# A forgetting-attention plus SwiGLU kernel: list-scheduled order, attention output with queries on partitions, q and k turned by DMA

## The chip, the cores and the metric

The kernel runs on one core of one Trainium2 chip. The metric is the device time of one execution in microseconds (us). The profile is one execution recorded by the hardware profiler; its span, from the first to the last instruction, is 1.5 to 2.5 us shorter than the timed figure of the same execution. The granted clock is the share of the full TensorE clock that the profile records (0.5 is half clock). The engines are PE (matmul; PEld is its weight load, which overlaps PE), DVE (VectorE), ACT (ScalarE), POOL (GpSimd) and SP (SyncE, which here only issues DMAs). A run over 1.5% above the fastest run of its own kernel is called slow and left out of ratios.

## The reference, cut to what matters

```python
B, H, S, D = 8, 8, 576, 64                       # q, k, v: float32, (B, H, S, D)
scores = q @ k^T / sqrt(D)
cum    = cumsum(log(clip(f, 1e-4, 1)))           # f: (B, H, S), 0.8 to 1.0
scores = where(causal, scores + cum[i] - cum[j], -1e9)
attn   = softmax(scores)
x      = (attn @ v) as (B*S = 4608 tokens, H*D = 512)
out    = (silu(x @ w_gate) * (x @ w_val)) @ w_out   # 512 -> 1536 -> 512, float32 weights
```

q and k are drawn with a scale of 0.1, so q.k/8 has a standard deviation of about 0.1 x 0.1 x 8 / 8 = 0.01, while one step of `cum` averages about 0.1. The scores are therefore almost all decay.

## The kernel before

Each head is scored in four slots; keys lie on partitions in the scores, so `pt = exp(scores)` is already the right operand for attention times V. V is stationary and `pt` moves. The output has the 64 features of a head on partitions plus a 65th row, the row sum (V carries columns of ones). Since the sum of a query then lies in a row, dividing by it needs it on 64 partitions: for most heads it travels by DMA, is inverted, goes out to DRAM and comes back broadcast. For the first 256 queries of batch 0 PE turns it in f32.

```python
def transposes(p, nm):                  # q and k of every pair of heads: six PE transposes each
    for n in range(QT):
        nc.tensor.transpose(t[:, n * QP : n * QP + P], src[:, n], ident)

def straighten(p, nm, a, eng):          # then four copies per pair, on ACT or DVE
    ...

def pv(h, i):                           # V stationary (128x128), up to 320 columns of pt move
    for n, (kt, q0, w) in enumerate(BANKS[i]):
        nc.tensor.matmul(o[:, q0 - q_lo : q0 - q_lo + w], VB[b][:, kt, j, :], PT[h, half][:, c : c + w], ...)
    ...
    if on_act: nc.scalar.activation(dst, o[: D + 1, :q_n], AF.Copy)
    else:      nc.vector.tensor_copy(dst, o[: D + 1, :q_n])

def collect(x, g, lo, n):               # the row sums of four heads onto 128 partitions
    nc.scalar.dma_start(out=SC[x][:, :c], in_=E[g][D : D + 1, ...])
def recip(x, n):   nc.vector.reciprocal(...)
def back(x, n):    nc.scalar.dma_start(out=rc_dram[...], in_=RC...)
def spread(x, n):  nc.scalar.dma_start(out=RB[x]..., in_=rc_dram[...].to_broadcast([D, GH * n]))
def normalise(x, h, lo, n):
    nc.vector.tensor_mul(xT[...], E[g][:D, c : c + n], RB[x][...])
... (cut: loads, casts on POOL, decay rows, exp, mask)

for h in range(BH):                     # a fixed order by slots; FFN matmuls are dealt out between them
    for i in range(NSLOT):
        at(slot(h, i), qk, h, i)
        ...
```

The score matmul has 68 rows of contraction: 64 of q and k, and four rows that carry the decay (`cum` in pieces that bfloat16 can hold, and ones).

The softmax here doesn't subtract the row's maximum and nothing guards it: scores larger than these inputs give would overflow.

## Time and profile before

| | before |
|---|---|
| median of 4 runs | 451.49 us (451.31 to 451.66) |
| span of the profiled run | 449.0 us |
| PE / DVE / ACT / POOL busy | 93 / 64 / 59 / 39% |
| sum of all matmuls at full rate | 391.9 us |
| loss (span less that sum) | 57.1 us |

The first lines are from the page of the kernel before: busy time by engine, then two of the rows that cut the span into 40 slices of 11.2 us. A digit is a busy share in tenths; DMA is the busy share of the 16 DMA engines.

```profile
PE 418.1 (93%) x2818; PEld 248.2 (55%) x2818; DVE 289.1 (64%) x523; ACT 267.1 (59%) x551; POOL 174.6 (39%) x409
...
PE   8399587899899899999999999999999999999996
...
DMA  9899960762818644942594359425912222200201
```

PE stands at 8 or 9 tenths from the eighth slice to the last but one. The second fence is from the timeline of PE, at 253 us: start, length, line, shapes, number of matmuls.

```profile
253.42 0.50 PE L135 MATMUL tp<-ident,b_q 128*128 128x128 bf16 x6
253.76 0.59 PE L311 MATMUL fo<-wo,hh 128*128 128x512 bf16 x2
```

Six matmuls of 128 columns start at 253.42 and the next group starts 0.34 us later: 57 ns each (55.6 on average in full streaks; a 512-column matmul takes 215.7). The Trainium skill ("TensorE: Matmul & The Clock Gate", Back-to-back issue gap) gives N/2.4 + 2.5 ns for a warm, isolated gap; this trace agrees with that formula, with about 2.2 to 2.4 ns as the constant. So the cost of PE work at full clock can be written down from its columns alone. I call the sum of columns/2.4 + 2.2 ns over all matmuls, dummies left out and four times the columns for f32, the matmul sum. (The four is an assumption. The 16 f32 transposes of 128 columns ran at half clock, with 214 ns from the first to the second of each pair, which would be twice the columns. Counted so, the sum before is 1.7 us smaller and the loss before 1.7 us larger.) What the span has beyond the sum is the loss: waits, half clock, start and end. The cumulative loss at a time is that time less the matmul sum of what had started by then.

Next, the busy time of each engine by window (window, length, PE busy with its instruction count, then the other engines; at the end granted clock, DMA share, GB/s), and two steps of the chain of waits that ended last, cut to the first 60 us (start, length, what).

```profile
20.00:40.00 20.00, 18.53 (x111) 12.29 (x110) 11.30 (x31) 10.03 (x21) 10.49 (x23) 0.56 1.18 208
40.00:60.00 20.00, 14.14 (x123) 10.71 (x121) 9.24 (x21) 11.36 (x24) 12.38 (x28) 0.91 1.17 210
```

```profile
41.40 11.44 DMA nat_q<-in_q_dram
52.92 6.87 DMA sc<-ev
```

By 80 us the loss is already 41.8 us of 57.1. From 20 to 60 us the DMA share is above 1 (the profile adds up the times of packets, so it can pass 1), and the chain steps through loads and then the 6.87 us of the row sums' DMA.

Last, groups of instructions from the page: line, engine, operation, output<-inputs, shapes, count | busy us, mean ns | idle time before, and what ended it.

```profile
L166 PE MATMUL s<-QK 68*128 68x320 bf16 (+4 forms) x448 | 88.5, 268 | 8.8 <-DMA QK<-dec_d 5.8
...
L198 PE MATMUL o<-pt,VB 128*128 128x320 bf16 (+4 forms) x448 | 88.0, 267 | 5.6 <-DVE QK L144 2.6
...
L219 DVE COPY ev<-o 65x320 f32<-65x320 f32 (+1 forms) x68 | 32.5, 478 | 42.2 <-PE o L198 42.1
...
L142 ACT ACTIVATE QK<-tp 64x576 bf16<-64x576 bf16 x66 | 42.6, 645 | 13.5 <-DMA nat_q<-in_q_dram 4.0
```

L166 are the scores, L198 attention times V, L219 half of the evictions of its output (the copies of a matmul's output from its PSUM tile to SBUF), L142 half of the straightening copies after the PE transposes.

### The profile page before, as it was taken

Reading aid. Unit: us, or ns where it says so; the run is one execution under the profiler, and the core shown is the slowest. Engines: PE = TensorE matmul, PEld = TensorE weight load, DVE = VectorE, ACT = ScalarE, POOL = GpSimd, SP = SyncE. Lnnn points to the kernel's source line nnn. Section 1 sums busy time; section 2 is a strip of 40 time slices with the busy share of each in tenths; the row PEclk is TensorE's granted clock in tenths of the full one; section 3 lists DMA queues with packets and bytes.
Section 4 is the critical chain, followed back from the end, with each engine's and each line's share of the span. In section 5 each row is a group of like instructions: output and inputs, shape, how many; then the busy total and the mean of one; then the engine's idle time right before and its main releaser. Section 6 shows DMA issues by size and latency. Waiting matters only on the chain.

```text
span 449.0 us, 8044 instructions
## 1 busy us (share of the span) xinstructions
PE 418.1 (93%) x2818; PEld 248.2 (55%) x2818; DVE 289.1 (64%) x523; ACT 267.1 (59%) x551; POOL 174.6 (39%) x409
## 2 busy tenths in 40 slices
PE   8399587899899899999999999999999999999996
PEld 3256465676766565555555555555555554444562
DVE  6464466585866875797379737973796479386280
ACT  5446466666667778776677667766776643233231
POOL 7855654334245646444444444444444310000000
PEclk9758999999999999999999999999999999999999
DMA  9899960762818644942594359425912222200201
GB/s 210 175 231 202 223 142 12 196 142 49 193 55 197 149 110 131 213 95 70 154 208 99 69 155 205 102 70 153 207 29 64 88 54 54 85 10 1 93 2 70
DMA packets 70195, 53.52 MB, mean 119 GB/s; under 512 B 45834, under 2 KB 64266, under 8 KB 69322
## 3 DMA queue, kind: packets, MB, share of 16 engines
q1 hardware_dynamic: 57626, 38.94, 35.0%
q10 hardware_dynamic: 6704, 9.34, 8.9%
q0 software_dynamic: 5824, 4.72, 6.8%
q8 instruction: 22, 0.36, 0.4%
q14 instruction: 19, 0.16, 0.1%
HBM read 47.38 MB, written 10.17 MB: 128 GB/s over the span
## 4 chain that ended last, share of the span: by engine, by line
PE 75%; DMA 9%; DVE 7%; ACT 4%; issue 2%; SPq 1%; ACTq 1%; POOL 0%; DVEq 0%; POOLq 0%
PE fo L311 20%; PE gp L293 18%; PE vp L302 18%; PE o L198 8%; PE s L166 8%; PE tp L135 4%; DMA nat_q<-in_q_dram 3%; DMA nat_v<-in_v_dram 3%; DVE th L296 2%; DVE xT L274 2%; DMA sc<-ev 2%; DVE hh L304 1%; ACT th L295 1%; ACT QK L142 1%; ACT pt L172 1%
## 5 line engine op out<-in xcount | busy, mean ns | idle before, releaser
L172 ACT ACTIVATE pt<-s 128x384 bf16<-128x384 f32 (+2 forms) x256 | 127.6, 502 | 77.1 <-PE s L166 72.0
L181 POOL TENSOR_SCALAR_AFFINE_SELECT pt<-pt 128x128 bf16<-128x128 bf16 (+2 forms) x256 | 83.8, 328 | 180.3 <-ACT pt L172 177.1
L302 PE MATMUL vp<-xT,wv 128*128 128x512 bf16 (+2 forms) x528 | 125.4, 341 | 1.4 <-DVE hh L304 1.4
L293 PE MATMUL gp<-xT,wg 128*128 128x512 bf16 (+2 forms) x528 | 125.9, 342 | 0.8 <-DVE th L296 0.5
L296 DVE SCALAR_TENSOR_TENSOR th<-th,gp 128x512 f32<-128x512 f32 (+2 forms) x132 | 77.5, 587 | 66.6 <-ACT th L295 63.6
L311 PE MATMUL fo<-wo,hh 128*128 128x512 bf16 x432 | 107.2, 379 | 0.8 <-DVE th L296 0.8
L166 PE MATMUL s<-QK 68*128 68x320 bf16 (+4 forms) x448 | 88.5, 268 | 8.8 <-DMA QK<-dec_d 5.8
L295 ACT ACTIVATE th<-gp 128x512 f32<-128x512 f32 (+2 forms) x132 | 68.3, 517 | 47.1 <-PE gp L293 39.0
L198 PE MATMUL o<-pt,VB 128*128 128x320 bf16 (+4 forms) x448 | 88.0, 267 | 5.6 <-DVE QK L144 2.6
L304 DVE TENSOR_TENSOR hh<-th,vp 128x512 bf16<-128x512 f32 (+2 forms) x132 | 77.5, 587 | 9.3 <-PE vp L302 0.7
L166 PEld LDWEIGHTS <-QK 68*128 68x128 bf16 x448 | 44.4, 101 | 49.4 <-issue 8.1
L302 PEld LDWEIGHTS <-wv 128*128 128x128 bf16 x528 | 49.3, 98 | 33.5 <-issue 2.4
L293 PEld LDWEIGHTS <-wg 128*128 128x128 bf16 x528 | 49.4, 98 | 32.2 <-issue 1.2
L219 DVE COPY ev<-o 65x320 f32<-65x320 f32 (+1 forms) x68 | 32.5, 478 | 42.2 <-PE o L198 42.1
L311 PEld LDWEIGHTS <-hh 128*128 128x128 bf16 x432 | 39.3, 97 | 35.6 <-issue 1.2
L144 DVE COPY QK<-tp 64x576 bf16<-64x576 bf16 x62 | 46.6, 752 | 17.7 <-PE tp L135 16.9
L198 PEld LDWEIGHTS <-VB 128*128 128x128 bf16 x448 | 39.2, 98 | 23.2 <-issue 4.9
L142 ACT ACTIVATE QK<-tp 64x576 bf16<-64x576 bf16 x66 | 42.6, 645 | 13.5 <-DMA nat_q<-in_q_dram 4.0
L274 DVE TENSOR_TENSOR xT<-ev,rb 64x576 bf16<-64x576 f32 (+2 forms) x72 | 48.6, 675 | 2.9 <-DMA rb<-rc_d 1.9
L314 ACT ACTIVATE ot<-fo 128x512 f32<-128x512 f32 x36 | 21.5, 596 | 29.9 <-PE fo L311 28.3
L122 POOL CAST b_q<-nat_q 96x768 bf16<-96x768 f32 x32 | 27.1, 846 | 6.7 <-DMA nat_q<-in_q_dram 6.7
L122 POOL CAST b_k<-nat_k 96x768 bf16<-96x768 f32 x32 | 27.0, 843 | 0.9 <-DMA nat_k<-in_k_dram 0.9
(49 smaller groups left out, 176.2 us busy)
## 6 DMA issues: line engine op xcount, KB each, us to landing
nat_q<-in_q_dram SPq DMA_DIRECT2D x32, 288.0 KB, 3.8
nat_k<-in_k_dram SPq DMA_DIRECT2D x32, 288.0 KB, 4.2
out_dram<-ot SPq DMA_DIRECT2D x36, 256.0 KB, 2.1
nat_v<-in_v_dram SPq DMA_DIRECT2D x64, 128.0 KB, 5.7
rb<-rc_d ACTq DMA_DIRECT2D x12, 576.0 KB, 6.8
wg<-in_moe_w_gate_dram POOLq DMA_DIRECT2D x4, 384.0 KB, 13.2
wv<-in_moe_w_val_dram POOLq DMA_DIRECT2D x4, 384.0 KB, 15.2
wo<-in_moe_w_out_dram POOLq DMA_DIRECT2D x4, 384.0 KB, 9.6
```

The costliest lines, as they stand in the source:

```text
L122: nc.gpsimd.tensor_copy(BF[nm, p % 2][:QP].rearrange("p t h d -> p h t d"), nat.pop((nm, p)).rearrange("p h (t d) -> p h t d", d=D),)
L166: nc.tensor.matmul(s[:, c : c + w], QK[b][:, 2 * j + 1, kt * P : (kt + 1) * P], QK[b][:, 2 * j, q0 : q0 + w], start=True, stop=True,)
L172: nc.scalar.activation(pt[:, off : off + c], s[:, :c], AF.Exp, scale=0.125)
L181: nc.gpsimd.affine_select(out=diag, in_=diag, pattern=pat, compare_op=ALU.is_ge, fill=0.0, base=0, channel_multiplier=-1,)
L198: nc.tensor.matmul(o[:, q0 - q_lo : q0 - q_lo + w], VB[b][:, kt, j, :], PT[h, half][:, c : c + w], start=(i <= 1 and n == 0), stop=(last a ...
L274: nc.vector.tensor_mul(xT[a * D : (a + 1) * D, (h % H) // 2, b0 : b0 + n], E[g][:D, c : c + n], RB[x][:, j * n : (j + 1) * n])
L293: nc.tensor.matmul(g_[:, :n], wg[:, ko, fs], xT[:, ko, ts], start=(ko == 0), stop=(ko == KD - 1))
L295: nc.scalar.activation(th[:, :n], g_[:, :n], AF.Tanh, scale=0.5)
L296: nc.vector.scalar_tensor_tensor(out=th[:, :n], in0=th[:, :n], scalar=1.0, in1=g_[:, :n], op0=ALU.add, op1=ALU.mult)
L302: nc.tensor.matmul(v_[:, :n], wv[:, ko, fs], xT[:, ko, ts], start=(ko == 0), stop=(ko == KD - 1))
L304: nc.vector.tensor_mul(h_[:, :n], th[:, :n], v_[:, :n])
L311: nc.tensor.matmul(o[:m], hh[fc][:, m0 : m0 + m], wo[:, fc, :], start=(fc == 0), stop=(fc == KF - 1))
```

## The change

The intent is fewer columns through PE and less work around it. Attention times V gets its operands swapped: a 128x128 block of probabilities is stationary and 65 columns of V (64 and ones) move. As before, blocks above the diagonal are not computed. The output then has queries on partitions and the row sum as a column, so a reciprocal and a broadcast multiplication on DVE normalise it with no DMA. The price is five PE transposes per pair of heads to bring x back to features on partitions. q and k of batches 2 to 7 are cast to bfloat16 by a DRAM-to-DRAM DMA (issued by POOL, `narrow`) and turned by 96 DMA transposes (issued by SP, `turned`; called crossbar transposes here), in place of POOL casts and PE transposes. A list scheduler (`Plan`) simulates engines, buffers and DMA with modelled durations at build time, and fixes the order of each engine's instructions. The diff is cut to its core and condensed; the comments are added here.

```diff
-for h in range(BH):                       # slots
-    for i in range(NSLOT):
-        at(slot(h, i), qk, h, i)
+class Plan:                               # list scheduler: heap of events, one queue per engine
+    def op(self, eng, fn, after=(), take=(), use=(), key=0.0, ready=0.0, dma=None): ...
+    def run(self, idle=None):
+        ...
+        lanes = [0.0] * 8                 # DMAs of SP and ACT in flight
... (cut)
-def transposes(p, nm): ...                # for every pair of heads
+def narrow(e, b, x):                      # batches 2 to 7, f32 -> bf16, DRAM to DRAM
+    nc.gpsimd.dma_start(out=qk_dram[2 * b + x, :HSD]..., in_=(q, k)[x][b]...)
+def turned(e, p, j, x):                   # each row: 64 values of its token, 64 of what follows
+    src = bass.AP(qk_dram.tensor, qk_dram.offset + lo, [[D, S], [1, P]])
+    nc.sync.dma_start_transpose(out=QK[:, hqk[p].i, 2 * j + x, :S], in_=src)
+def rows(e, p):                           # decay rows then overwrite partitions 64 to 67
+    E[e].dma_start(out=QK[D:KR, hqk[p].i, :, :S], in_=dec_dram[:, 2 * p : 2 * p + 2]...)
... (cut)
-nc.tensor.matmul(o[:, q0 - q_lo : q0 - q_lo + w], VB[b][:, kt, j, :], PT[h, half][:, c : c + w], ...)
+for n, (kt, qb, c) in enumerate(cells):   # 15 cells per head
+    lo = base + qb * (D + 1)
+    nc.tensor.matmul(o[:, lo : lo + D + 1], pt[:, c : c + P], VB[hvb[b].i][:, kt, hb, : D + 1], ...)
-def collect / recip / back / spread / normalise   # row sums by DMA
-def turn / turn_back                              # row sums by f32 PE transposes
+def invert(e, bo, br, n):
+    nc.vector.reciprocal(RC[br.i][:, :n].unsqueeze(2), o[:, :, D:])
+def scale(e, bo, br, bx, j, qb, nq):
+    nc.vector.tensor_mul(XN[bx.i][...], o, r)          # r: the reciprocal, broadcast over 64 columns
+def flip(e, bx, bt, qb, nq):
+    for n in range(nq):
+        nc.tensor.transpose(t[:, n * P : (n + 1) * P], XN[bx.i][:, qb + n]..., ident)
... (cut: buffers now share xT and wo; decay rows of batches 0 and 1 by four DMAs, one per row)
+W_AT = [15.0, 19.0, 36.0, 42.0]           # planned times at which weights are fetched
```

## The prediction

> **What bounds the kernel now.** TensorE. The page gives PE 93% busy against DVE 64%, ACT 59%, POOL 39%, and the chain that ended last is 75% PE. From 200 to 430 us PE is never idle (busy time by windows) and the matmuls stand back to back: starts in the timeline are 215.7 ns apart at 512 columns, 138 at 320, 55.6 at 128, 28 at 64. That is N/2.4 GHz plus about 2.3 ns[...]; weight loads are hidden, also behind 64 columns. That spacing summed over all matmuls but the 18 dummies gives 392 us of the 449 us span. The other 57 us are lost to waits and half clock: 42 us in the first 80 us (DMA-bound: about 205 GB/s at share 0.9 to 1.2; clock 0.5 to 0.6 from 20 to 40 us), 10 us from 80 to 200 us, about 5 us at the end.
>
> **What the change does to PE.**
> - Attention times V: the probabilities become stationary, V with its ones column moves. Per head 15 matmuls of 65 columns replace 7 of 1600 columns in all: at 29 to 31 ns each 0.45 us against 0.69 us. 64 heads: 44 to 29 us, -15 us.
> - q and k transposes: 384 to 96 of 128 columns, 55.6 ns each: -16 us.
> - New output transposes, 160: +9 us. The f32 turns for row sums vanish: -7 us.
> - 37 output tiles instead of 36: +2.6 us. Scores and gates unchanged (45 and 187 us).
> Sum: 392 to about 368 us, all critical while PE is dense.
>
> **Off PE.** ACT loses the evictions of o (21 us) and most straightening copies; DVE loses 31 us of evictions and most of 47 us of copies, gains reciprocals, scales and xT copies (my estimate 65 us). Both stay under 70%. POOL loses 48 of 64 q/k casts. DMA gains 12 DRAM-to-DRAM casts (1.2 MB read each) and 96 crossbar transposes of 147 KB (14 MB). The skill ("Advanced Engine Details and Errata", X-Bar Transpose) calls those as fast as ordinary DMAs; no run here shows it. The DMA share after 90 us is 0.1 to 0.9, so there is room, and attention leads the FFN, so a late transpose has slack.
>
> **Ramp.** The bytes needed first (q, k, v of two batches, weights) are the same, so it stays DMA-bound. The row-sum chain goes (a 6.9 us wait in the chain at 53 us), and a list order fills gaps. I expect 48 us of loss instead of 57. The static order rests on modelled durations, slightly short for ACT (0.55 us modelled, 0.595 measured at 512 columns); small PE waits are in that.
>
> **Prediction.** Span 368 plus 48 to 51, plus 2.4 us by which the timed run exceeds the profile: 420 us; 8 in 10 between 409 and 437. Faster by over 2%: 0.91, within 2%: 0.06, slower: 0.03.
>
> **Right or wrong in the profile.** The 65-column matmuls' starts 28 to 32 ns apart; PE full from about 100 us to the end; about 24 us less warm matmul work; loss before 80 us of 35 to 42 us; the last pairs' transposes landing before PE wants them.
>
> **What would make it wrong.** Runs of up to nine 65-column matmuls, each with its own weight load, going at 55 ns (+23 us: then within 2%); crossbar transposes taking several us of queue or DMA each, so scores wait for QK after 100 us; a static order that blocks PE behind exp, mask or the single o and t banks.

## The result, and the profile after

The kernel after takes 425.21 us (median of 4 runs, 423.55 to 428.66) against 451.49 us. The ratio is 0.9424, with a 95% interval of 0.9381 to 0.9466. Here and below a ratio is the mean time of one kernel's fast runs over that of the other's in the same rounds, so not quite the ratio of the medians. The result is correct. The change is faster by about 5.8%.

The same page lines of the kernel after (slices of 10.6 us):

```profile
PE 388.1 (91%) x3071; PEld 227.5 (54%) x3114; DVE 230.3 (54%) x438; ACT 215.1 (51%) x442; POOL 126.9 (30%) x351
...
PE   3626999989999869999999999999999999999996
...
DMA  9994799966693798569959959975401002001002
```

| | before | after |
|---|---|---|
| span of the profiled run, us | 449.0 | 424.4 |
| matmul sum, us | 391.9 | 368.1 |
| loss, us | 57.1 | 56.3 |
| first score matmul at, us | 13.2 | 35.9 |
| cumulative loss at 40 / 80 / 140 / 160 us | 27.7 / 41.8 / 47.8 / 50.5 | 35.2 / 41.0 / 42.6 / 50.1 |

(The trace of the kernel after lacks 43 of the FFN's matmul records. The sum takes them from the program, so it is not affected; PE's busy figure is.)

So of the 24.6 us that the span lost, 23.8 are matmul columns that are no longer there, and only 0.8 are saved waiting (22.1 and 2.5 with f32 at twice the columns). That the loss hardly changed is partly luck, for gains and losses of several us cancel in it. Within the loss there is movement: the new kernel loses 7.5 us more in the first 40 us, 12.7 us less from 40 to 140 us, and 4.8 us more from 140 to 160 us. Two new problems can be seen in the PE row: the digits 3, 6, 2, 6 at the start, and the single 6 in the fifteenth slice, at about 150 us; the kernel before has no digit under 8 between its seventh slice and its last.

The windows of the kernel after:

```profile
20.00:40.00 20.00, 7.50 (x70) 5.80 (x68) 6.24 (x11) 5.84 (x14) 3.23 (x7) 0.61 0.67 119
40.00:60.00 20.00, 18.91 (x246) 15.20 (x245) 14.04 (x34) 18.01 (x45) 12.96 (x39) 0.88 0.94 171
...
120.00:160.00 40.00, 34.97 (x320) 20.82 (x323) 16.82 (x36) 22.64 (x48) 14.93 (x44) 0.97 0.81 132
```

From 20 to 40 us PE did 7.50 us of work, against 18.53 before (part of which was at half clock and on row sums), while the DMA share fell to 0.67 from 1.18. The start is no longer limited by bytes. From 40 us on it recovers: 18.91 us of PE work in the next 20 us against 14.14. That fits a list order that finds work and row sums that nobody waits for, but no run separates the two, and work put off from the first 40 us was ready too.

Two groups of attention times V on the page of the kernel after (some of it reads another tile, PTa, and stands in another group), and then groups of PE's timeline at 152 us:

```profile
L512 PE MATMUL ps<-VB,PT 128*128 128x65 bf16 x768 | 47.3, 195 | 3.7 <-POOL PT L498 3.7
L512 PEld LDWEIGHTS <-PT 128*128 128x128 bf16 x768 | 39.4, 99 | 19.1 <-POOL PT L498 4.8
```

```profile
151.78 0.43 PE L512 MATMUL ps<-VB,PT 128*128 128x65 bf16 x9
152.05 0.55 PE L481 MATMUL ps<-QK 68*128 68x192 bf16 x4
...
157.13 0.27 PE L512 MATMUL ps<-VB,PT 128*128 128x65 bf16 x3 [3.66 <-POOL PT L498]
```

The mean of 195 ns in the group line is the length of one matmul from issue to modelled end, and does not tell the rate. The starts do: nine matmuls of 65 columns start at 151.78 and the next group at 152.05, so 30 ns each. Over all streaks after 60 us the median is 29 ns and the mean 31. Every one of these has a weight load of 128 columns of its own (L512 PEld: mean 99 ns), and those are hidden. The last line shows the other thing: until 157.13 PE waited 3.66 us for a causal mask on POOL (4.2 us between the starts of two weight loads; PE gaps below are measured so).

**Where the start went.** This is the chain of waits of the kernel after, cut to its first 40 us:

```profile
2.37 5.94 DMA xT<-in_q_dram
...
8.79 1.50 DVE xT L307
...
18.71 7.50 DMA QK<-xT
26.23 0.57 ACTq L341
...
27.48 8.31 DMA QK<-xT
...
35.92 2.08 PE ps L481 x12
```

The DVE memset of line 307 fills three rows of ones for the decay. It starts only once a q load has landed (2.37 + 5.94 = 8.31). Both write parts of the same tile, whose space is borrowed for scratch; their bytes do not meet, but the memset's box of three strided rows spans the load's addresses, so it was made to wait. After it a row of small DVE operations runs until 18.6. Then the first of four decay-row DMAs takes 7.50 us, and the second is issued only when the first has landed (18.71 + 7.50 = 26.21, next issue 26.23). I infer from the eight lanes that the scheduler reckons with that these two share a completion semaphore; what the trace shows is the wait. The second round takes another 8.31 us, and the first score starts at 35.92.

**Where 150 us went.** This is the chain of the same kernel from 140 to 165 us, then POOL's timeline, then SP's queue of DMA issues (where the length is the time that the issuing instructions took):

```profile
146.03 10.07 DMA natv<-in_v_dram
156.22 0.61 POOL VB L284
156.83 0.25 POOL PT L498
```

```profile
147.10 0.53 POOL L382 DMA_DIRECT2D qk_d<-in_q_dram  x1
...
148.59 0.53 POOL L382 DMA_DIRECT2D qk_d<-in_k_dram  x1
...
156.22 0.61 POOL L284 CAST VB<-natv 128x512 bf16<-128x512 f32 x1 [5.30 <-DMA natv<-in_v_dram]
```

```profile
146.03 0.40 SPq L400 DMA_DIRECT2D natv<-in_v_dram  x1
146.48 15.34 SPq L391 DMA_TRANSPOSE QK<-qk_d  x4
```

A V load issued at 146.03 lands at 156.10, after 10.07 us (the kernel before has a median of 5.7 for V, with loads of half the size). POOL's cast of that V tile waits 5.30 us, behind it in POOL's order stands the mask, which runs at 156.83, and behind the mask stands PE. Just after the load's issue POOL issued two DRAM-to-DRAM casts, at 147.10 and 148.59. The four crossbar issues on SP from 146.48 on take 15.34 us together (1.4, 2.5, 8.6 and 2.7), where the median of all 96 is 1.26. The first of them began before the casts; the long ones came after. The clock record adds a part: from 157.4 to 160.9 us, 3.4 us long, the granted clock is half. The Trainium skill ("TensorE: Matmul & The Clock Gate", What's actually happening) says that the array falls to half clock after an idle window of about 3.4 us; a gap of 4.2 us between weight loads, from 152.9 to 157.1, and 3.4 us at half clock right after it agree with that. But such a gap is not needed: e0, the same kernel run again, has no such gap (see the experiments) and yet is at half clock for 6.8 us from 148.3; in the ten us before, no idle gap between its matmuls is over 0.7 us.

### The profile page after: what moved, and what is told of

It reads as the page before. It is cut to its first block, busy times and chain, and to the rows that moved or that the text cites. A ratio compares the mean times of both kernels' runs of the same rounds, so it can differ in the third digit from the quotient of the medians.

```text
span 424.4 us, 8314 instructions
## 1 busy us (share of the span) xinstructions
PE 388.1 (91%) x3071; PEld 227.5 (54%) x3114; DVE 230.3 (54%) x438; ACT 215.1 (51%) x442; POOL 126.9 (30%) x351
## 3 DMA queue, kind: packets, MB, share of 16 engines
q1 hardware_dynamic: 105120, 38.65, 44.8%
## 4 chain that ended last, share of the span: by engine, by line
PE 84%; DMA 7%; DVE 3%; ACT 3%; issue 1%; SPq 0%; ACTq 0%; POOL 0%; DVEq 0%; POOLq 0%
PE ps L613 42%; PE ps L628 22%; PE ps L481 10%; PE ps L512 7%; DMA QK<-xT 4%; DMA natv<-in_v_dram 2%; PE ps L536 2%; DMA xT<-in_q_dram 1%; ACT PT L489 1%; ACT QK L282 1%; DVE QK L284 1%; DVE xT L329 0%; ACT th L617 0%; PE ps L374 0%; DVE xT L307 0%
## 5 line engine op out<-in xcount | busy, mean ns | idle before, releaser
L613 PE MATMUL ps<-xT,wv 128*128 128x512 bf16 (+3 forms) x466 | 112.7, 359 | 0.7
L613 PE MATMUL ps<-xT,wg 128*128 128x512 bf16 (+3 forms) x471 | 111.5, 357 | 0.5
L621 DVE SCALAR_TENSOR_TENSOR th<-th,ps 128x512 f32<-128x512 f32 (+3 forms) x120 | 75.5, 629 | 64.2 <-ACT th L617 64.1
L617 ACT ACTIVATE th<-ps 128x512 f32<-128x512 f32 (+3 forms) x120 | 66.5, 555 | 83.0 <-PE ps L613 79.8
L489 ACT ACTIVATE PT<-ps 128x512 bf16<-128x512 f32 (+2 forms) x192 | 92.5, 510 | 28.2 <-PE ps L481 20.9
L628 PE MATMUL ps<-wo,hh 128*128 128x512 bf16 (+1 forms) x424 | 103.5, 379 | 1.0
L481 PE MATMUL ps<-QK 68*128 68x320 bf16 (+4 forms) x448 | 76.9, 271 | 7.1 <-DMA QK<-xT 5.3
L624 DVE TENSOR_TENSOR hh<-th,ps 128x512 bf16<-128x512 f32 (+3 forms) x120 | 75.9, 634 | 12.8 <-PE ps L613 0.8
L498 POOL TENSOR_SCALAR_AFFINE_SELECT PT<-PT 128x128 bf16<-128x128 bf16 (+1 forms) x192 | 52.7, 277 | 76.2 <-ACT PT L489 70.7
L512 PE MATMUL ps<-VB,PT 128*128 128x65 bf16 x768 | 47.3, 195 | 3.7 <-POOL PT L498 3.7
L512 PEld LDWEIGHTS <-PT 128*128 128x128 bf16 x768 | 39.4, 99 | 19.1 <-POOL PT L498 4.8
L481 PEld LDWEIGHTS <-QK 68*128 68x128 bf16 x448 | 36.1, 101 | 20.2 <-issue 8.3
L632 ACT ACTIVATE ot<-ps 128x512 f32<-128x512 f32 (+1 forms) x37 | 22.1, 597 | 47.1 <-PE ps L628 46.4
L489 ACT ACTIVATE PTa<-ps 128x384 bf16<-128x384 f32 x64 | 30.7, 492 | 24.6 <-PE ps L481 24.4
L284 DVE COPY xT<-ps 128x576 bf16<-128x576 bf16 (+1 forms) x30 | 13.2, 441 | 14.3 <-PE ps L536 12.9
```

Of the source, the lines that this page charges most:

```text
L284: E[e].tensor_copy(dst, src)
L481: nc.tensor.matmul(s[:, c : c + w], QK[:KR, hqk[p].i, 2 * j + 1, kt * P : (kt + 1) * P], QK[:KR, hqk[p].i, 2 * j, q0 : q0 + w], start=True ...
L489: nc.scalar.activation(place(h, i)[:, OFFS[i] : OFFS[i] + c], ps(bs)[:, :c], AF.Exp, scale=0.125)
L498: nc.gpsimd.affine_select(out=d, in_=d, pattern=pat, compare_op=ALU.is_ge, fill=0.0, base=0, channel_multiplier=-1,)
L512: nc.tensor.matmul(o[:, lo : lo + D + 1], pt[:, c : c + P], VB[hvb[b].i][:, kt, hb, : D + 1], start=first and n == 0, stop=last and n == l ...
L613: nc.tensor.matmul(ps(bf)[:, :n], w[:, ko, fc * P : (fc + 1) * P], xT[:, ko, t0 : t0 + n], start=(ko == 0), stop=(ko == KD - 1))
```

## The experiments

Twelve kernels ran: eleven edits of the kernel after, and as e0 that kernel itself. Three further sets of runs of the kernel before gave 451.47 us (beside e1 to e4), 451.81 (e5, e6, e8, e9) and 451.62 (e0, e10 to e12). All gave "correct". The accounting for all of them follows; sum, span and loss are of the profiled run alone. Where that run was slow (marked *), its span and loss can't be compared with those of fast runs. In e1, e5 and e6 it was the fastest of the four; elsewhere it lies anywhere in the range.

| kernel | median us (range) | ratio to before | matmul sum | span | loss |
|---|---|---|---|---|---|
| before | 451.49 (451.31–451.66) | 1 | 391.9 | 449.0 | 57.1 |
| after | 425.21 (423.55–428.66) | 0.9424 | 368.1 | 424.4 | 56.3 |
| e0, after again | 422.97 (422.30–424.13) | 0.9372 | 368.1 | 422.4 | 54.3 |
| e1, more transposes | 447.96 (443.33–449.17) | 0.9892 | 384.1 | 441.6 | 57.5 |
| e2, weigh twice | 453.92 (452.04–454.75) | 1.0029 | 396.2 | 452.9 | 56.6 |
| e3, plain copies | 422.71 (421.00–423.03) | 0.9345 | 368.1 | 421.3 | 53.2 |
| e4, extra ACT, planned | 437.89 (434.36–441.25) | 0.9662 | 368.1 | 438.0 | 69.9 |
| e5, e1 in the same order | 444.01 (441.55–444.97) | 0.9819 | 384.1 | 439.8 | 55.7 |
| e6, extra ACT, same order | 429.80 (426.93–431.45) | 0.9506 | 368.1 | 425.2 | 57.1 |
| e8, start of the kernel | 417.81 (413.17–427.28) | 0.9216 | 368.1 | 415.8 | 47.6 |
| e9, V loads earlier | 436.75 (431.47–441.67) | 0.9617 | 368.1 | 439.8* | 71.7* |
| e10, no casts | 420.53 (418.22–421.19) | 0.9306 | 368.1 | 419.0 | 50.9 |
| e11, e8 with a V-cast lag | 420.14 (412.64–424.84) | 0.917 | 368.1 | 418.8* | 50.7* |
| e12, e11 with casts in halves | 414.04 (412.11–418.54) | 0.9172 | 368.1 | 416.8* | 48.7* |

The theory was that the gain is the matmul sum alone, and that all of it counts because PE is the limit. The rivals were that relief of ACT and DVE, or the vanished row-sum DMAs, made the gain, and that the crossbar transposes gave some of it back.

### Is PE time all that counts? (e2, e1, e5)

e2 issues every 65-column matmul twice (the sum is then doubled in both the output and the ones column, so the result stands):

```diff
-            nc.tensor.matmul(
-                o[:, lo : lo + D + 1], pt[:, c : c + P], VB[hvb[b].i][:, kt, hb, : D + 1], ...
+            for twice in range(2):
+                nc.tensor.matmul(
+                    o[:, lo : lo + D + 1], pt[:, c : c + P], VB[hvb[b].i][:, kt, hb, : D + 1], ...
... (the planner is told of twice the time)
```

> Every 65-column matmul of the attention-times-V product is issued twice, weight load and all; sums and weighted values both double, so the result stays right. Theory (29.3 ns for each, its weight load hidden): 960 x 29.3 ns = 28 us more, 453 us, 449 to 458. If a 128-column weight load really costs about 55 ns that the short matmul can't hide in longer streaks: over 470 us. Rival (slack on TensorE): below 435 us.

It took 453.92 us. The matmul sum rose by 28.1 us and the span of the profiled run by 28.5; the total loss did not move (56.3 to 56.6). Its parts did, since the planner chose another order: 36.1 us at 80 us against 41.0, and some 10 us between 250 and 300 us, where a V load took 12.32 us to land and PE waited 5.9 us for a mask. So the exact match is in part luck. The mean spacing in streaks was 30.3 ns with twice as many weight loads, so these do not limit here. This also answers the first danger that the prediction named.

e1 puts back the PE transposes that the crossbar had taken over, as twelve extra ones per pair:

```diff
-        for n in range(nq):
+        for n in range(nq if p < FIRST * FB else nq + 12):
+            n = n % nq
... (the planner is told of the added time)
```

> 288 more transposes of 128 columns on TensorE (12 for each of the 24 pairs of heads of batches 2 to 7), the number that the change took off it; the crossbar DMAs stay and the result stays right. Theory (the gain is matmul time taken off a TensorE that is never short of work, one for one): 288 x 55.6 ns = 16.0 us more, so 441 us, 438 to 445. Rival (the gain came from the order, from the row-sum DMAs that went, or from relief of ScalarE and VectorE, and TensorE has slack): below 431 us.

It took 447.96 us, and the range of 443.3 to 449.2 is wide. That is 22.7 us more for 16.0 us of matmuls, more than the theory allows. Because the planner was told, it chose another order. That this order met the DMA casts at worse moments is my guess; the only profile is of the fastest run, whose span rose by 17.2 us, and it does not show the excess. e5 is the same edit of `flip` with the planner kept ignorant, so the order of instructions is that of the kernel after:

> The 288 extra transposes of the first experiment again, but the list scheduler is not told of them, so every instruction keeps its place in its engine's order. Theory (matmul time counts one for one; the first experiment cost more than its 16 us because the new order met the DMAs at other moments): 438 to 444 us. Rival (28 columns of extra time come from something else that these transposes do, such as holding the PSUM bank): 446 us or more, as before. Below 431 us: TensorE has slack.

It took 444.01 us, at the upper edge of what was expected: 18.8 us over the first runs of the kernel after and 21.0 over its repeat. In the profiled runs the span rose by 15.4 us for 16.0 us of matmuls, and the loss was 55.7; but the profiled run of e5 was the fastest of its four, that of the kernel after its third. By the medians a microsecond of PE time cost 1.2 to 1.3. So PE has no slack to hide 16 us, and the rival is out. Whether the cost is one for one or somewhat more stays open; the medians of these kernels scatter by 2 to 3 us.

### Is relief of ACT worth anything? (e4, e6)

e4 adds one ACT eviction of each attention output to a scratch tile, known to the planner.

```diff
+    def evict(e, bo, n):
+        nc.scalar.activation(SCRATCH[:, : n * (D + 1)], ps(bo)[:, : n * (D + 1)], AF.Copy)
+                extra = [op(("ACT", act(g * (D + 1))), evict, bo, g, after=ws + ..., use=[bo], key=kk - 1, ...)]
```

> ScalarE copies each head's output out of PSUM once more, to a scratch tile that nobody reads: about 72 copies, some 28 us of ScalarE, as much as the evictions and half of the straightening copies that the change took off it. Theory (ScalarE is off the critical path): at most 3 us more, 424 to 428 us. Rival (relief of ScalarE is part of the gain): over 432 us.

This missed: 437.89 us. It does not show that ACT is the limit. The trace has a new stall: crossbar issues of 11.1 us (at 154, just after casts at 151 and 154) and 6.5 us (at 165) on SP, PE gaps of 3.0 us at 167 and 5.5 us at 177, and in the latter a wait of 4.9 us for decay rows that stood behind them on SP. The cumulative loss goes from 52.7 at 160 us to 63.0 at 200 us. A replanned order had moved onto the same trouble. How much of the excess that is and how much the ACT work, this run can't say. e6 therefore adds ACT work outside the plan, 64 copies from one scratch tile to another:

```diff
+        if i == 3:
+            nc.scalar.activation(SCRATCH[:, :400], SOURCE[:, :400], AF.Copy)
```

> One more ScalarE copy of 128x400 per head, SBUF to SBUF, waiting for nobody and read by nobody, 64 in all, about 28 us of ScalarE; the scheduler is not told, so the order stays. Theory (ScalarE has slack; the 12 us of the fourth experiment came of its new order): 424 to 428 us. Rival (ScalarE's relief is part of the gain, its work adds to the critical path): over 432 us.

It took 429.80 us, just outside the expected range. ACT's busy time rose by 23.7 us (215.1 to 238.8) and the time by 4.6 us over the first runs of the kernel after and 6.8 over its repeat; the intervals of the ratios do not overlap (0.9474 to 0.9537, against 0.9381 to 0.9466 and 0.9348 to 0.9396). The profiled run, the fastest of them, has a loss of 57.1, hardly more. Why ACT work costs that much I have not found. Relieving ACT of 52 us (267.1 to 215.1) may have bought something: in proportion it would be 10 to 15 us, an estimate from these two figures that no run tests, and such a gain would have to be hidden in the loss by what the start and other stalls cost. The relief of DVE (289.1 to 230.3 us busy) was not tested at all.

### The stall at 150 us: crossbar, casts, or V loads? (e3, e10, e9)

e3 replaces each crossbar transpose by an ordinary copy of the same bytes (wrong; it passes only because q and k hardly count here, as worked out above):

```diff
-        src = bass.AP(qk_dram.tensor, qk_dram.offset + lo, [[D, S], [1, P]])
-        nc.sync.dma_start_transpose(out=QK[:, hqk[p].i, 2 * j + x, :S], in_=src)
+        src = bass.AP(qk_dram.tensor, qk_dram.offset + lo, [[280, P], [1, S]])
+        nc.sync.dma_start(out=QK[:, hqk[p].i, 2 * j + x, :S], in_=src)
```

> The 96 crossbar transposes become ordinary DMAs of the same 147 KB from the same DRAM buffer to the same place, on the same queue (the q and k of batches 2 to 7 are then not turned: wrong result on purpose). Theory 1 (the stall of some 8 us at 150 us, where a queue of three crossbar transposes takes 12.6 us and the next v load lands late, comes of the crossbar): no such stall, 415 to 420 us. Theory 2 (any 14 MB would do that, or the casts from DRAM to DRAM do it): 423 to 428 us as before.

It took 422.71 us, between the two theories: 2.5 us under the first runs of the kernel after, and only 0.3 us under its repeat. The two were run in different rounds, so a cost of the crossbar in the time can't be told from scatter. It does cost in the queue. These are the lines of the main hardware queue (packets, MB, share of 16 engines) of the kernel after and of e3:

```profile
q1 hardware_dynamic: 105120, 38.65, 44.8%
```

```profile
q1 hardware_dynamic: 60576, 38.65, 36.0%
```

The same 38.65 MB take 44.8% instead of 36.0% of the DMA engines, and an issue takes 1.26 us instead of 0.43. But in e3 something holds SP as well, as its issue timeline shows:

```profile
148.67 2.05 SPq L391 DMA_DIRECT2D QK<-qk_d  x4
150.81 11.83 SPq L400 DMA_DIRECT2D natv<-in_v_dram  x4
```

Four issues of ordinary V loads take 11.83 us. So it is not the crossbar alone. e10 takes the casts away instead: only batch 2 is cast, and all later batches turn batch 2's copy (again wrong):

```diff
-        lo = (2 * b + x) * (HSD + D) + h * S * D
+        lo = (2 * FIRST + x) * (HSD + D) + h * S * D
... (narrow is replaced by a one-element memset on POOL for b > FIRST; the order stays)
```

> The DRAM-to-DRAM casts of q and k run for batch 2 alone; for batches 3 to 7 a tiny memset stands in their place in GpSimd's order, and the crossbar turns batch 2's copy again (wrong result on purpose; every engine's order stays). Theory (the long crossbar issues of 4 to 9 us on the SP queue, which hold the v loads behind them, come only while a cast is in flight, crossbar and cast together): no crossbar issue over 3 us after 120 us, no TensorE stall over 2 us after 100 us, 418 to 423 us, as with plain copies. Rival (the crossbar queue stalls by itself): long issues stay, 423 to 428 us.

It took 420.53 us, as expected. Its SP timeline at the same place:

```profile
146.46 5.60 SPq L394 DMA_TRANSPOSE QK<-qk_d  x4
152.16 3.00 SPq L403 DMA_DIRECT2D natv<-in_v_dram  x4
```

The same four crossbar issues take 5.60 us instead of 15.34, the longest of all is 2.3 us, and PE has no gap over 1.5 us after 100 us. The cumulative loss at 160 us is 44.7 against 50.1 us.

The fairer comparison is e0, the kernel after unaltered, in the same rounds as e10. These are its PE row, its four issues and a window of it:

```profile
PE   3545999989999999999999999999999999999996
```

```profile
146.97 11.58 SPq L391 DMA_TRANSPOSE QK<-qk_d  x4
```

```profile
150.00:155.00 5.00, 4.78 (x27) 2.59 (x26) 1.64 (x4) 2.29 (x5) 2.17 (x6) 0.50 1.02 123
```

Its four issues take 11.58 us, but the same V load had landed by 153.02, 6.5 us after its issue, and PE has no gap over 1.5 us after 100 us either; nor has e3, with its casts. So PE's wait of 3.66 us is what one execution met, not what the order always brings. e0 loses 5.3 us from 140 to 160 us all the same, in good part at half clock (0.50 in the window shown), against about 2 in e10. What e10 shows is that crossbar issues of over 3 us come with DRAM-to-DRAM casts in flight (the longest is 8.6 us in the first profile, 4.9 in e0) and not without them, and that the time is 2.4 us less than e0's in the same rounds. That late V loads follow from such issues and then stop POOL and PE is a chain read from traces: the first profile and e2 have it, and e9 below. How the casts hold SP (which resource) the runs do not show.

e9 tried a remedy: V loads issued 8 us earlier, their casts on POOL placed 10 us later in the plan.

```diff
-            values(b, n, 1000 * b + n, ready=release(p) - 12 + n)
+            values(b, n, 1000 * b + n, ready=release(p) - 12 - 8 + n, lag=10)
```

> The v loads of batches 2 to 7 go out 8 us earlier, and the scheduler places their casts on GpSimd no sooner than 10 us after the load (it assumed about 2.5 us), so that a late load no longer holds GpSimd and the masks behind it. Theory (the stall at 150 us is TensorE waiting for a mask that stands behind a cast that waits for a v load): no stall over 2 us after 100 us, 417 to 421 us. Rival (the crossbar queue itself starves the scores): 424 to 428 us.

This missed badly: 436.75 us, and its runs took 431 us or more. The profile is of a slow run (441.67 us), so the lengths below may be greater than in the others. The issue queue of SP and then POOL at 220 us, in e9:

```profile
221.32 12.71 SPq L400 DMA_DIRECT2D natv<-in_v_dram  x4
```

```profile
219.88 0.53 POOL L382 DMA_DIRECT2D qk_d<-in_q_dram  x1
...
234.19 0.61 POOL L284 CAST VB<-natv 128x512 bf16<-128x512 f32 x1 [11.60 <-DMA natv<-in_v_dram]
```

The V loads now fall right onto the casts. Their issue takes 12.71 us, POOL waits 11.60 us, and PE stands for 9.9 us from 225 (and for 3.6 us at 194 and 2.8 us at 278). The chain from V load to cast, mask and PE is seen again, in the wrong direction. What matters is not how early a load is placed but what it meets.

### The start (e8), and a better version (e11, e12, e0)

e8 mends the start: one memset per row, so that none spans a load; decay rows on SP ahead of the later V loads; the bulk of the decay rows for later batches held back.

```diff
-            nc.vector.memset(dec[:, 1:, 0], 1.0)
+            for r in (1, 2, 3):
+                nc.vector.memset(dec[:, r, 0], 1.0)
-        o_row.append(op(("ACT", 0.5), row, r, after=a, key=-9, dma=0.15))
+        o_row.append(op(("SP", 0.5), row, r, after=a, key=-9, dma=0.15))
-    o_decd = op(("SP", SPi), dec_out, after=[o_up, o_lo, o_dec[0], o_dec[1]], key=60, dma=2.0)
+    o_decd = op(("SP", SPi), dec_out, after=o_row, key=60, dma=2.0, ready=30.0)
... (V loads 2 to 4 of batch 0 wait for o_row; xT copies of batch 0 need not wait for the scratch)
```

> The start alone: the memset of the ones rows of dec becomes three, so that it no longer waits for q and k loads; the four decay rows go out on the SP queue before the later v loads and get semaphores of their own, so that none waits for the landing of another; the copy of the other rows to DRAM is put off to 30 us. Theory (the first 40 us are lost because the scores wait until 35.9 us for the decay rows, not because bytes are missing): first scores at 18 to 25 us, loss before 80 us 27 to 34 us instead of 41, time 411 to 418 us. Rival (the start is bound by the bytes of q, k, v and weights, as the prediction had it): scores earlier, but the loss comes back by 80 us, 421 us or more.

It took 417.81 us, 7.4 us under the first runs of the kernel after and 5.2 under its repeat (neither in the same rounds). Its chain at the start, and its window from 20 to 40 us:

```profile
3.31 0.54 DVE xT L308
...
11.33 1.05 DVE xT L338
12.40 8.45 DMA QK<-xT
20.99 0.80 PE ps L482 x4
```

```profile
20.00:40.00 20.00, 18.54 (x209) 14.70 (x210) 10.20 (x25) 15.74 (x38) 13.00 (x35) 0.66 1.08 208
```

The memset starts at 3.31 instead of 8.79, there is one round of decay DMAs instead of two, and the first score starts at 20.99 instead of 35.92. PE does 18.54 us of work in the window where it did 7.50, at a DMA share of 1.08. So the start of the kernel after was a chain of waits and not a matter of bytes. Scores start 15 us earlier, but the loss at 40 us is only 9.1 us less (26.1 against 35.2), since part of that window runs at half clock (0.66 granted) and still has gaps; of those, 8.7 us remain at the end of the profiled run (6.7 against that of e0). Two of its six runs were slow, one of them at 427 us; this scatter I cannot explain.

e11 adds to e8 only a later place for V's casts on POOL (11 us after the load's planned time), so that a late V load does not block masks. e12 adds that each DRAM-to-DRAM cast goes in two halves, 9 us apart.

```diff
... (both: as e8)
+            eng, cast_v, b, n, bv, after=[o, o_vb[b % NVB]], use=[bv], key=key, ready=ready + lag,   # lag=11
... (e12 also)
-    def narrow(e, b, x):
+    def narrow(e, b, x, half):
+        lo, hi = half * HSD // 2, (half + 1) * HSD // 2
-                prev_narrow[b] = [op(("POOL", SW), narrow, b, x, ..., ready=release(p) - 12, dma=3.5, ...) for x in range(2)]
+                prev_narrow[b] = [[op(("POOL", SW), narrow, b, x, half, ..., ready=release(p) - 14 + 9 * half,
+                                       dma=1.8, ...) for half in range(2)] for x in range(2)]
```

> The early start of the eighth experiment, and the scheduler places the v casts of batches 2 to 7 no sooner than 11 us after the load was free to go; the loads stay where they were, unlike in the ninth experiment, where they were moved onto the casts of q and k. Theory: GpSimd no longer stands before a mask for a late v load, 412 to 417 us with less spread than the eighth. Rival (in the eighth the casts already came at harmless moments): 416 to 419 us, the same.

> As the eleventh, and each DRAM-to-DRAM cast is cut into two of half the size, 9 us apart. Theory (the bursts of casts block the SP queue in proportion to their size): crossbar issues no longer than 4 us, 410 to 416 us. Rival (any cast in flight blocks it, so twice as many blocks of half the length): within 2 us of the eleventh.

e11 gave no gain that can be told from scatter: 412.64 to 424.84 us, and four of six runs were slow, so that its ratio of 0.917 rests on two. Its profiled run, a slow one, has a PE gap of 5.4 us at 211 us, waiting for decay rows. e12 took 414.04 us (412.11 to 418.54), five of six runs fast, ratio 0.9172 (0.9135 to 0.9209). In its profile, of its one slow run, the longest crossbar issue is 5.2 us, where 4 or less was expected, but the others are at most 3.7. By the ratios of fast runs e12 and e11 are the same, so the rival is not excluded; what differs is that more of e12's runs were fast. By the median it is the best version: 8.3% under the kernel before, and 2.1% under the kernel after in the same rounds (414.04 against 422.97).

e0 is that control: the kernel after, unchanged, beside e10 to e12.

> The changed kernel itself, unaltered, on the chip and in the rounds of the next three, to have its own spread beside them: 423 to 429 us as in the first runs; it has no theory to tell apart.

It took 422.97 us, 2.2 us under its first result and just under the range expected. Differences of 2 or 3 us between different rounds are therefore not to be read.

## Why the prediction was right or wrong, point by point

The prediction was 420 us, 409 to 437; the result was 425.21. The direction and the size were right, and so was the main term, the fall of the matmul sum. The time was low by 5 us, and that error is in one term, the loss. One figure came out right by luck; it is named below.

- **The matmul sum falls from 392 to 368 us: right.** It is 391.9 and 368.1, and it accounts for 23.8 of the 24.6 us of the span. The listed items add up to -26, not -24: the f32 turns stand there with 7 us, the sum counts 3.5, and their spacing in the trace would give 1.7. e2 and e5 show that added PE work costs about its full time or somewhat more (28.5 us of span for 28.1; 18.8 to 21.0 us by the medians for 16.0).
- **65-column matmuls at 29 to 31 ns, weight loads hidden: right.** The median is 29 and the mean 31 ns; also with twice as many (30.3).
- **The term that was mis-sized: "I expect 48 us of loss instead of 57".** It measured 56.3 us (54.3 in the repeat). The range given for the first 80 us, 35 to 42, held at 41.0; after that a total of 48 to 51 left room for 7 to 10 us, and 15.3 were lost.
- **"PE full from about 100 us to the end": wrong in one place,** a gap of 4.2 us and 3.4 us at half clock around 150 us. Together with what surrounds it, the stretch from 140 to 160 us lost 7.5 us. In the repeat the gap was absent and the stretch lost 5.3 us; without casts (e10) it lost 2.1 us.
- **"The bytes needed first are the same, so it stays DMA-bound": wrong as a reason.** The DMA share was 0.67 from 20 to 40 us, and scores waited for four small DMAs until 35.9 us. e8 showed 6.7 to 8.7 us of the loss to lie there. The number for the first 80 us came out all the same, by luck: from 40 to 80 us only 5.8 us were lost against 14.1 before.
- **"The row-sum chain goes, and a list order fills gaps": supported, not isolated.** From 40 to 140 us the loss is 7.4 us against 20.1, but no run separated the two reasons.
- **Crossbar transposes in time: right, with a warning.** In the kernel after the waits of PE name no crossbar tile. But their room was judged by DMA share ("there is room"), and what ran short was the issue queue of SP. The prediction had named "several us of queue" as a danger, and it came true, in the first profile, for a V load rather than for scores.
- **Relief of ACT and DVE, which the prediction counted as no gain: not settled.** "Both stay under 70%" is right (51 and 54%). But e6 puts 4.6 to 6.8 us on 23.7 us of ACT, so ACT's work is not free, and no run tried DVE.

## What to carry to other kernels

When PE is full, count columns: the operand that moves pays for its width, so a matmul whose output is narrow on one side should move that side (here 29 to 31 ns for 65 columns against about 139 for 320). Here the span fell by about what the matmul sum fell. A change that takes work from the bottleneck still moves what starts when, so read the first 40 us and the stretches around large background DMAs on their own: an engine that waits for one late load stops what is placed behind it, as POOL's 5.30 us did, and a DMA's cost is also what it does to the issue queue beside it. To cost one part of a statically scheduled kernel, keep the order of instructions fixed; e4 and perhaps e1, which let the planner choose anew, measured the new order beside the added work. And profile the unaltered kernel a second time before you explain a stall: the one at 150 us was there in one of two profiles.

## What the Trainium skill lacked or had wrong

- "TensorE: Matmul & The Clock Gate", Back-to-back issue gap, says that in a real kernel with a weight load per matmul the spacing is about 81 ns at 128 columns and 131 ns at 512, and that N/2.4 + 2.5 ns holds only for an isolated gap. The "isolated" formula holds in full streams with a weight load each: 55.6 ns at 128, 215.7 at 512, 29 to 31 at 65. (Its section "Wait — 56ns, not 53.3ns?" gives 55.6 and 215.7 ns back to back, as here, so the page disagrees with itself.)
- The same page, LDWEIGHTS, gives P/1.2 ns, by which I estimate 107 ns for the 128 columns loaded here; the trace has a mean of 97 to 104 ns in the large groups. It has no case of such loads hidden behind matmuls of 29 ns, as 960 in the kernel after and 1,920 in e2 were.
- "Advanced Engine Details and Errata", X-Bar Transpose (TRN2), says that transpose DMAs are as fast as regular ones. For the same bytes an issue took 1.26 us against 0.43 for a plain copy, and the queue's share was 44.8% against 36.0%. In the time of the kernel the difference (0.3 or 2.5 us) was within the scatter between rounds.
- "DMA: Bandwidth & Descriptors", Issuing engines are not separate DMA queues, says that transfers of all issuing engines share the DMA engines, and that issue time is usually small. It does not say that issues on SP can take long while DRAM-to-DRAM casts from POOL are in flight: 8.6 us for one crossbar issue (at most 2.3 without later casts, in e10), 11.83 and 12.71 us for four plain loads.
- No page gives a time near that of the decay rows, DMAs of 36 KB each to one partition, beside other traffic: 7.50 us from issue to landing for the first, 8.31 for the last of the three after it, and 8.45 for the last of the four in e8.
